# Pooled attention and a gated feed-forward in one program: sums of keys and values as one VectorE reduction, the last operands split on VectorE alone, tile 0's output by column halves, and an order that knows the shared SBUF port

## The chip, the cores and the metric

The kernel runs on one core of one Trainium2 chip. A core has TensorE (PE, matrix products into PSUM), VectorE (DVE), ScalarE (ACT), GpSimd (POOL, which has no access to PSUM here) and SyncE (SP, which issues the transfers). The metric is the device time of one execution in microseconds; smaller is better.

## The reference

```python
q, k, v: (8, 8, 576, 64) float32            # batch, heads, sequence, head dimension
k_p = k.reshape(B, H, 72, 8, D).mean(axis=3)  # keys and values pooled by 8
v_p = v.reshape(B, H, 72, 8, D).mean(axis=3)
scores = scale * q @ k_p.transpose(0, 1, 3, 2)
attn = softmax(scores)
x = (attn @ v_p) -> (4608, 512)              # tokens, heads x head dimension
g = x @ w_gate; val = x @ w_val              # (512, 1536) each
out = (g * sigmoid(g) * val) @ w_out         # (1536, 512)
```

All inputs and the output are float32. The weights come in as 64-bit floats and are turned into 32-bit ones on the chip. Products in 16-bit types run on a high part and a low part of each operand (three products for one).

## The kernel before

**Tiles and pieces.** The 4608 tokens form nine tiles of 512. The attention works on 40 pieces of at most 128 tokens of one batch. Tile 0 has pieces 0 to 3 and tile 1 pieces 4 to 8; batch 0 gives pieces 0 to 4.

**Keys and values.** Batch 0 is pooled on its own (keys by a reduction on VectorE, L405, values by products with a unit matrix, L510). For the batches 1 to 7, six parts each are loaded (`kv_part`, 576 KB, L1161), and GpSimd adds the eight addends of each result in three halving additions (L1169 to L1171). `prep` then scales and splits the values.

**A piece** (`answer`): scores on TensorE (L587), row maxima on VectorE (L594) and their scaled negative (`biases`, L598), eight exponentials on ScalarE with a running sum each (L606), the reciprocal (L613 to L616), a high part on ScalarE and a low part on GpSimd (`soft_low` L639 or `blocks_low` L649), a DMA transpose, the product with the values (L658 to L661 or L668 to L674), division (L678), again a high part on ScalarE and a low part on GpSimd (L1336), and a DMA transpose into the tile's x.

**Weights.** Each of twelve chunks of gate and value weights is decoded (`chunk`): a shift (L340), the sign (`w_sign`, on VectorE L352, GpSimd L347 or ScalarE L354), magnitude (L359), joining (L363), sums (L374), and a high and a low part (L389, L394).

**Steps.** A tile takes twelve steps, one per chunk. A plain step (`plain_step`, L771 to L773) multiplies 512 columns by both weights. A fast step (`fast_step`, L875) uses seven products of quarter blocks instead of eight, with 256 columns; it needs sums of weight blocks (`fast_weights`, L796 to L815) and of x (`fast_x`, L836 to L844). Tiles 0 and 1 are plain; from tile 2 on a chunk goes fast once its sums are made. The gate's tanh (L718) and two VectorE products (L721, L726) end a step, and the result goes to memory (L899).

**The output product** comes after the last tile. The intermediate comes back in blocks (L1469) and the product with `w_out` runs for pairs of tiles with seven products, called 1 to 7 (`last_products`), each of 2 x 18 matmuls of 512 columns: 6 with float32 operands rounded for the array (L1589) and 12 in bfloat16 with the low parts (L1603, L1604). Their left operands come from `operands`: block sums on VectorE (`less`, L1500, four sums of three parts each), and a cut of each operand into a rounded copy on ScalarE (L1486) and a low part (L1490), of which two parts of three are made on GpSimd and one on VectorE. Tile 0, the odd one, comes first (`single_operands`, `single_products`): four plain products of 2 x 18 matmuls.

**The order.** The order on every queue (TensorE, VectorE, ScalarE, GpSimd, SP) is written by a planner (`Order`) while the program is built. Every line of work is a generator that yields operations with an engine and a cost in ns, transfers with due times, buffers it takes (`get`) and puts back (`put`), and flags. The planner takes, of the operations that can start first, the one of the highest rank. Ranks come from a kind and a number; `CHUNK_RANK`, `KV_RANK`, `PIECE_RANK` and `VALUES` are such numbers for the beginning. The chip runs each queue in that order and waits where an operand is not ready.

Of the kernel before, what the change touches and what calls it, by code (L numbers as in the profile page):

```python
# [8 lines left out]
F16 = mybir.dt.float16  # L9
# [8 lines left out]
P = 128  # L18
# [5 lines left out]
LAG = 4  # L24
# [12 lines left out]
SIGN_AS_INT = (2, 4, 8, 9)  # L37
SIGN_ON_POOL = (5, 11)
# [28 lines left out]
class Order:  # L67
# [26 lines left out]
    def ready(self, e):  # L94
        return max(e["need"][4], self.pipe - self.HOLD if len(e["need"]) > 6 else 0)
# [50 lines left out]
    def run(self):  # L146
        while self.lines:
# [3 lines left out]
            for engine, free in self.free.items():  # L151
                ops = [e for e in self.lines if e["need"][0] == "op" and e["need"][1] == engine]
# [13 lines left out]
            _, engine, ns, f, _, *times = e["need"][:6]  # L166
            self.now = max(self.now, at)
# [27 lines left out]
def attention_then_swiglu(  # L195
# [71 lines left out]
    nc.gpsimd.memset(shares[:, 1:2], 1.0 / POOLW)  # L267
    least = const.tile([P, 4], F32, name="least")
# [73 lines left out]
    def w_sign(c):  # L342


        ws, high = chunks[c]["ws"], chunks[c]["high"]
        if c in SIGN_ON_POOL:
            nc.gpsimd.tensor_single_scalar(  # L347
                ws.bitcast(F16)[:, :, 1], high.bitcast(F32), 2.0**-60, ALU.mult
            )
        elif c in SIGN_AS_INT:  # L350
# [259 lines left out]

    def one_over(b, n, sm):
# [141 lines left out]
    def f_room(name):  # L753
# [7 lines left out]
            "hf": ["hf0", "hf1", "hh0", "hh1"], "rs": [0, 1], "f": [f_own], "xc": [(early, "early")],  # L761
# [23 lines left out]
    def fast_weights(c):  # L785

        if True:
            t = yield flag(("used", 1, c))
# [7 lines left out]
            t = yield op("DVE", 1280, lambda: nc.vector.tensor_add(f, g_h, g_l), t, t0)  # L796
# [23 lines left out]
    def fast_x(i):  # L820
# [9 lines left out]
        if i in SUMS_ON_POOL:  # L830
            on, eng, cost = nc.gpsimd, "POOL", (765, 1196)
# [972 lines left out]
```

## Time and profile before

| | us |
|---|---|
| median of 3 runs (lowest, highest) | 954.63 (953.04, 957.86) |
| the profiled execution | 950.87 |
| its span, first to last instruction | 948.8 |
| mean granted TensorE clock | 0.978 |
| first half step of tile 0 | 48.4 |
| first step of tile 1 | 143.6 |
| output product, from | 677 |

The span is the time from the first to the last instruction on the core. The share of busy time on the page is a mean over stages that differ much; the clock is what TensorE was granted, 1 being full. In a view by stretches, each row has the stretch, its length, the busy time and count for TensorE, its weight loads, VectorE, ScalarE and GpSimd, then the granted clock, the transfer engines' busy share and GB/s.

### The profile page before, as it was taken

What the parts mean: (1) busy time and instruction counts of PE and PEld (TensorE: products, weight loads), DVE (VectorE), ACT (ScalarE), POOL (GpSimd) and SP (SyncE); (2) the same over time, 40 slices, a digit from 0 to 9 for tenths busy, and PEclk for the clock granted to TensorE, in tenths of its full rate; (3) what the DMA queues carried; (4) which work ended last, traced back from release to release, by engine and by line L of the source; (5) the groups of instructions that cost most, each with busy time, mean ns of one, the idle gap of its engine ahead of it and who ended that gap; (6) DMA issues with size and microseconds to landing.
All of it is one profiled execution on the core that took longest, in us unless ns stands there. A gap on an engine that the chain in (4) does not pass through costs nothing. (4 is left out here: it accounts for less than half of the span.)

```text
span 948.8 us, 17997 instructions
## 1 busy us (share of the span) xinstructions
PE 887.7 (94%) x6687; PEld 628.9 (66%) x6687; DVE 666.6 (70%) x1016; ACT 539.4 (57%) x1408; POOL 584.0 (62%) x516
## 2 busy tenths in 40 slices
PE   4599889998999999998999999999899899999998
PEld 4486444445767887787888888888655455555554
DVE  5998966785885676865766655567737669496781
ACT  5899755553755664776676754455435345444442
POOL 3874997958829768648624513033547568677682
PEclk9699899999999999999999999999999899999999
DMA  9949974548359359469485543146450631706201
GB/s 328 329 144 277 249 168 102 127 132 194 83 163 184 104 137 261 119 164 252 103 170 142 127 123 112 67 145 234 178 176 3 224 131 54 289 12 251 104 23 67
DMA packets 138759, 148.38 MB, mean 156 GB/s; under 512 B 85808, under 2 KB 106288, under 8 KB 136368
## 3 DMA queue, kind: packets, MB, share of 16 engines
q1 hardware_dynamic: 138672, 147.24, 53.6%
q8 instruction: 52, 0.85, 0.4%
q14 instruction: 35, 0.29, 0.1%
HBM read 87.29 MB, written 40.89 MB: 135 GB/s over the span
## 5 line engine op out<-in xcount | busy, mean ns | idle before, releaser
L875 PEld LDWEIGHTS <-mixed 128*128 128x128 f16 x1404 | 136.4, 98 | 24.9 <-issue 5.5
L1603 PE MATMUL ps<-low,wsh 128*128 128x512 bf16 x384 | 146.7, 382 | 4.0 <-DVE low L1490 4.0
L875 PEld LDWEIGHTS <-wgv_h 128*128 128x128 f16 x1248 | 121.0, 98 | 32.5 <-issue 14.3
L875 PE MATMUL ps<-xc,mixed 128*128 128x256 f16 x936 | 123.2, 274 | 1.0 <-ACT ps L935 0.9
L875 PE MATMUL ps<-xc,wgv_h 128*128 128x256 f16 x624 | 109.6, 272 | 11.4 <-DVE ps L943 7.3
L721 DVE SCALAR_TENSOR_TENSOR hf<-hf,ps 128x512 f32<-128x512 f32 (+1 forms) x112 | 74.3, 664 | 63.0 <-ACT hf L718 62.6
L718 ACT ACTIVATE hf<-ps,un 128x512 f32<-128x512 f32 (+1 forms) x112 | 75.3, 672 | 72.3 <-PE ps L875 55.8
L606 ACT ACTIVATE sc<-ps,mx 128x72 f32<-128x72 f32 (+1 forms) x320 | 97.8, 330 | 22.2 <-DVE mx L598 19.4
L875 PE MATMUL ps<-x,wgv_h 128*128 128x256 f16 x624 | 109.2, 273 | 0.0
L726 DVE SCALAR_TENSOR_TENSOR hf<-ps,un,hf 128x512 f32<-128x512 f32 (+1 forms) x112 | 81.6, 729 | 37.8 <-PE ps L875 26.8
L771 PE MATMUL ps<-x,wgv_h 128*128 128x512 f16 (+1 forms) x272 | 98.3, 361 | 1.4 <-DMA x<-spare 1.4
L772 PE MATMUL ps<-x,wgv_h 128*128 128x512 f16 (+1 forms) x272 | 98.0, 360 | 0.5 <-DVE x L688 0.4
L773 PE MATMUL ps<-x,wgv_l 128*128 128x512 f16 (+1 forms) x272 | 97.8, 360 | 0.4 <-DVE wgv_l L394 0.3
L875 PE MATMUL ps<-x,wgv_l 128*128 128x256 f16 x312 | 85.1, 273 | 0.0
L875 PE MATMUL ps<-xc,wgv_l 128*128 128x256 f16 x312 | 85.0, 272 | 0.0
L649 POOL TENSOR_TENSOR half<-sc,half 128x448 f16<-128x448 f32 (+1 forms) x35 | 39.6, 1130 | 57.2 <-ACT half L644 51.2
L1490 POOL TENSOR_TENSOR low<-wgv_h,hs 128x1024 bf16<-128x1024 f32 x18 | 51.2, 2866 | 34.3 <-ACT hs L1486 34.3
L1603 PEld LDWEIGHTS <-wsh 128*128 128x128 bf16 x384 | 37.6, 98 | 51.5 <-issue 10.2
L1169 POOL TENSOR_TENSOR in<-in 128x576 f32<-128x576 f32 x42 | 62.3, 1483 | 13.8 <-DMA in<-kv_parts 13.8
L606 ACT ACTIVATION_READ_ACCUMULATOR sc<-ps,mx 128x1 f32 (+1 forms) x320 | 69.4, 217 | 0.0
L875 PE MATMUL ps<-x,mixed 128*128 128x256 f16 x468 | 64.1, 273 | 3.3 <-DVE ps L938 3.3
L875 PEld LDWEIGHTS <-wgv_l 128*128 128x128 f16 x624 | 61.0, 98 | 7.2
(189 smaller groups left out, 2095.3 us busy)
## 6 DMA issues: line engine op xcount, KB each, us to landing
hd<-hf SPq DMA_DIRECT2D x104, 256.0 KB, 2.3
in<-kv_parts SPq DMA_DIRECT2D x42, 576.0 KB, 5.4
ws<-w_all SPq DMA_DIRECT2D x36, 512.0 KB, 5.2
wgv_h<-hd SPq DMA_DIRECT2D x9, 1536.0 KB, 6.8
wgv_l<-hd SPq DMA_DIRECT2D x9, 1536.0 KB, 9.3
out_t<-ob SPq DMA_DIRECT2D x36, 256.0 KB, 3.8
qt<-q_rows SPq DMA_DIRECT2D x32, 256.0 KB, 3.5
wd<-wf SPq DMA_DIRECT2D x12, 256.0 KB, 2.4
```

The source lines that it names most:

```text
L606: nc.scalar.activation(sc[:n, h], pss[g][:n, j * SP : (j + 1) * SP], AF.Exp, bias=mx[:n, g, j : j + 1], scale=EXPSCALE, accum_out=sm[:n, h ...
L649: nc.gpsimd.tensor_sub(a[:, :, SP:], sc[:n, :, : P - SP], a[:, :, : P - SP])
L718: nc.scalar.activation(hf, gate, AF.Tanh, scale=un[:, c, 0:1])
L721: nc.vector.scalar_tensor_tensor(out=hf, in0=hf, scalar=1.0, in1=gate, op0=ALU.add, op1=ALU.mult)
L726: nc.vector.scalar_tensor_tensor(out=out, in0=val, scalar=un[:, c, 2:3], in1=hf, op0=ALU.mult, op1=ALU.mult)
L771: nc.tensor.matmul(o, wh, x["h"][:, j, a:e], start=(j == 0), stop=False)
L772: nc.tensor.matmul(o, wh, x["l"][:, j, a:e], start=False, stop=False)
L773: nc.tensor.matmul(o, wl, x["h"][:, j, a:e], start=False, stop=(j == NJ - 1))
L875: nc.tensor.matmul(o, a, b, start=begin and j + n == 0, stop=j == HJ - 1 and n == 2, skip_group_check=True,)
L1169: nc.gpsimd.tensor_add(a[:, :4], a[:, :4], a[:, 4:])
L1490: lambda: on.tensor_sub(low[:, 2 * n : 2 * n + 2], src[:, 2 * n : 2 * n + 2], rows[n].bitcast(F32)),
L1603: nc.tensor.matmul(o, top, where[1][:, c], start=False, stop=False, skip_group_check=True)
```

## The change

- **Sums of keys and values:** the three GpSimd additions of each of the 42 parts become one `tensor_reduce` on VectorE, and the host lays the eight addends next to each other.
- **Output operands:** all three low parts of every cut are made on VectorE.
- **Tile 0's output** goes through the same seven products as a pair, with its two column halves of 256 in place of the two tiles: 7 x 2 x 18 matmuls of 256 columns. Its operands share the two buffer sets by halves (`SLOT`). The first pair starts with product 3, which then has a bank of its own (`joined`).
- **The planner** treats VectorE operations marked `DVE+` and all GpSimd operations as exclusive of one another, and many costs are changed.
- **Attention:** 12 of the 40 pieces (`WHOLE`) subtract the row maximum and sum the rows on VectorE and take all exponentials in one ScalarE instruction. 19 low parts of the weights of attention and 13 low parts of x move from GpSimd to VectorE; the normalisation of all pieces of batch 0 is on GpSimd.
- **Beginning:** the values' loads have a rank of their own ahead of the chunks; new ranks for chunks, pieces and batch 1; five chunks instead of four in half steps for tile 0; the sign of six chunks on VectorE (before four), four on ScalarE (before six), two on GpSimd by `tensor_mul`; products of zeros on TensorE until the first step.
- Three chunks' low parts of weight sums move to VectorE, and the `w_out` cuts on VectorE are 4, 6 and 7 instead of 1, 7 and 3. The bank of the value sums goes to the attention and comes back at piece 8, and one more bank is lent at the end.

```diff
-LAG = 4
+LAG = 5
-SIGN_AS_INT = (2, 4, 8, 9)
-SIGN_ON_POOL = (5, 11)
+SIGN = dict(enumerate("DAAADAPPDDDD"))
-CHUNK_RANK = 0.9, 0.3
+CHUNKS = (1.08, 1.4, 1.95, 2.49, 2.66, 3.05, 3.37, 3.55, 3.86, 3.92, 4.12, 5.22)
-SECOND = 2
-BANKS = "val"
-VALUES = 0.9
+SECOND = 1
+BANKS = "att"
+VALUES = 0.47
+V_LOAD = 0.54
+WV = 9
+WHOLE = (0, 1, 3, 20, 21, 24, 25, 26, 28, 31, 34, 35)
-KV_RANK = 1.4
-PIECE_RANK = 0, 0.5, 1.2, 1.3, 2.2, 2.8, 3.4, 4, 4.6
-ON_POOL = (3, 4, 5, 6, 7, 8, 9)
+KV_RANK = 2.57
+CUT_ON_DVE = 0, 1, 2
+WAYS = {-1: (1, 5, 6, 2, 7, 3, 4), 0: (3, 1, 5, 2, 6, 7, 4)}
+SLOT = (0, 0), (0, 1), (1, 0), (1, 1), (0, 0), (1, 0), (1, 1)
+PIECE_RANK = (-0.26, 0.03, 1.27, 0.72, 1.85, 3.34, 3.35, 3.98, 3.19)
+ON_POOL = (0, 1, 2, 3, 4, 5, 6, 7, 8, 9)
+LOW_ON_DVE = (0, 4, 7, 12, 14, 15, 16, 19, 21, 23, 24, 26, 27, 28, 29, 32, 35, 37, 38)
+XT_ON_DVE = (0, 2, 3, 6, 7, 10, 13, 21, 24, 27, 30, 33, 38)
+WEIGHTS_ON_DVE = (1, 2, 8)
+CUT_W_ON_DVE = (4, 6, 7)
-SLACK = {"PE": 50, "DVE": 100, "ACT": 100, "POOL": 200, "SP": 100}
+SLACK = {'PE': 50, 'DVE': 100, 'ACT': 450, 'POOL': 50, 'SP': 100}
...
     def ready(self, e):
-        return max(e["need"][4], self.pipe - self.HOLD if len(e["need"]) > 6 else 0)
+        at = e["need"][4]
+        if e["need"][1] in ("DVE+", "POOL"):
+            return max(at, self.port - 200)
+        return max(at, self.pipe - self.HOLD if len(e["need"]) > 6 else 0)
...
+            if engine in ("DVE+", "POOL"):
+                self.port = at + ns - 160
...
+    def less_max(n, pss, sc, g):
+        mx = small.tile([P, GH], F32, name="mx1")
+        pv = pss[g][:n, : GH * SP].rearrange("p (h s) -> p h s", h=GH)
+        nc.vector.tensor_reduce(out=mx[:n], in_=pv, axis=AX.X, op=ALU.max)
+        nc.vector.tensor_tensor(
+            out=sc[:n].rearrange("p (j g) s -> p g j s", g=2)[:, g], in0=pv,
+            in1=mx[:n].unsqueeze(2).broadcast_to([n, GH, SP]), op=ALU.subtract,
+        )
+    def all_exponentials(n, sc):
+        nc.scalar.activation(sc[:n], sc[:n], AF.Exp, scale=EXPSCALE)
+    def row_sums(n, sc, sm):
+        nc.vector.tensor_reduce(out=sm[:n], in_=sc[:n], axis=AX.X, op=ALU.add)
...
     def fast_weights(c):
-            t = yield flag(("used", 1, c))
+            t = yield flag(("used", FAST_FROM - 1, c))
+            t = max(t, (yield flag(("decoded", 9 + c // 3 if c < 9 else c, 1))))
...
+    def warm():
+        where, t = yield get("val")
+        zeros = const.tile([P, TILE], F16, name="zeros")
+        t = yield op("POOL", 300, lambda: nc.gpsimd.memset(zeros, 0.0), 0)
+        def products():
+            ps = bank(where)
+            for _ in range(2):
+                nc.tensor.matmul(ps, zeros[:, :P], zeros, start=True, stop=True)
+        while ("taken", 0, 0) not in order.flags:
+            t = yield op("PE", 430, products, t)
+        put("val", where, t)
...
-            part["in"] = buffer(mid, [P, POOLW, KV // 6], F32, "in", "mid", at=n)
+            part["in"] = buffer(mid, [P, KV // 6, POOLW], F32, "in", "mid", at=n)
...
         def add():
-            a = part["in"]
-            nc.gpsimd.tensor_add(a[:, :4], a[:, :4], a[:, 4:])
-            nc.gpsimd.tensor_add(a[:, :2], a[:, :2], a[:, 2:4])
-            nc.gpsimd.tensor_add(dst, a[:, 0], a[:, 1])
-        t = yield op("POOL", 2800, add, t, ready)
+            nc.vector.tensor_reduce(out=dst, in_=part["in"], axis=AX.X, op=ALU.add)
+        t = yield op("DVE", 1400, add, t, ready)
...
     def cut_operand(p, k, src, t):
-            th = yield op("ACT", 1043, lambda: nc.scalar.copy(rows[n], src[:, 2 * n : 2 * n + 2]), t, t0)
-            eng, ns, on = (("POOL", 3000, nc.gpsimd), ("DVE", 2000, nc.vector))[n == 2]
+            na, nd, ng = (1043, 1210, 2390) if p >= 0 else (620, 680, 1270)
+            th = yield op("ACT", na, lambda: nc.scalar.copy(rows[n], src[:, 2 * n : 2 * n + 2]), t, t0)
+            eng, ns, on = (("POOL", ng, nc.gpsimd), ("DVE+", nd, nc.vector))[n in CUT_ON_DVE]
...
     def operands(p):
-        b11, b12, b21, b22 = (block[h, n] for h in range(2) for n in range(2))
+        if p < 0:
+            b11, b12, b21, b22 = (block[0, h][:, :, n * HT : (n + 1) * HT] for h in range(2) for n in range(2))
+        else:
+            b11, b12, b21, b22 = (block[h, n] for h in range(2) for n in range(2))
...
     def last_products(p):
-        for k in (1, 5, 2, 6, 3, 7, 4):
+        js = range(2) if p >= 0 else range(1)
+        def sides(j, o):
+            return [(j, o)] if p >= 0 else [(i, o[:, i * HT : (i + 1) * HT]) for i in range(2)]
+        turns = WAYS.get(p, WAY)
+        alone = turns.index(3) < turns.index(6)
+        for k in turns:
...
                 elif k in (6, 7):
                     o[j] = s[j]
+                    if k == 7:
+                        t0 = yield flag(("begun", p, 3, j))
...
-    kv = kv.reshape(B - SPLIT, POOLW, P, 6, -1).transpose(0, 3, 2, 1, 4)
+    kv = kv.reshape(B - SPLIT, POOLW, P, 6, -1).transpose(0, 3, 2, 4, 1)
```

More of the change, by code (lines that the diff above doesn't have):

```diff
@@ L151, in run @@
             for engine, free in self.free.items():
-                ops = [e for e in self.lines if e["need"][0] == "op" and e["need"][1] == engine]
+                ops = [e for e in self.lines if e["need"][0] == "op" and e["need"][1].rstrip("+") == engine]
                 if not ops:
@@ L1449, in operand_room @@
         low = const.tile([P, HC, TILE], BF16, name="low", tag="wo2", bufs=1)
-        put("set", (rows, low), t)
+        sets.append((rows, low))
+        order.done(("set", 0), t)
         t = yield flag(("tile", len(tiles) - 1))
@@ L1454, in operand_room @@
         low = const.tile([P, HC, TILE], BF16, name="low", tag="mixed2", bufs=1)
-        put("set", (rows, low), t)
+        sets.append((rows, low))
+        order.done(("set", 1), t)
+        if MORE:
+            where, t0 = yield get("val")
+            put("gate", where, t0)
     def load_block(p, h, n):
@@ L1479, in load_single, with room_for @@
         order.done(("block", -1, 0, n), t)
+    def room_for(p, k):
+        if p >= 0:
+            where, t = yield get("set")
+            return where, t
+        at = WAYS[p].index(k)
+        i, side = SLOT[at]
+        t = yield flag(("set", i))
+        if at > SLOT.index((i, side)):
+            t = yield flag(("made", p, WAYS[p][SLOT.index((i, side))]))
+        cs = slice(side * HT, (side + 1) * HT)
+        rows, low = sets[i]
+        return ([a[:, :, cs] for a in rows], low[:, :, cs]), t
     def cut_operand(p, k, src, t):
-        where, t0 = yield get("set")
+        where, t0 = yield from room_for(p, k)
         rows, low = where
@@ L1542, in operands @@
+        for k in WAYS.get(p, WAY):
+            src, when, free = of[k]
+            t = yield from cut_operand(p, k, src, (yield when))
             order.done(("cut", p, k), t)
-            if free:
+            if k == 3 and p >= 0:
+                order.start(("cut", p), freed(p, t))
+            elif free and p >= 0:
                 order.done(("free", p, *free), t)
+        if p < 0:
+            order.done(("free", p, 0, 1), max(t, (yield flag(("cut", p, 3)))))
     def seeded(p, k, j, o, src, t, t0):
@@ L1654, in last_products @@
             o = {}
-            for j in range(2):
+            for j in js:
                 t0 = 0
@@ L1735, in all_lines @@
             order.start(("load", -1), load_single(n))
-        order.start(("cut", -1), single_operands())
-        order.start(("out", -1), single_products())
+        order.start(("cut", -1), operands(-1))
+        order.start(("out", -1), last_products(-1))
         for p in range((len(tiles) - 1) // 2):
```

301 lines of the change are left out of this document (170 added, 131 removed).

## The prediction

> **What bounds the kernel now.** I read the page first, then the engines' busy time by stage, the waits of TensorE, and single lines for prices.
>
> ```profile
> span 948.8 us, 17997 instructions
> ...
> PE 887.7 (94%) x6687; PEld 628.9 (66%) x6687; DVE 666.6 (70%) x1016; ACT 539.4 (57%) x1408; POOL 584.0 (62%) x516
> ```
>
> The profiled execution took 950.87 us, 2.1 around its span; the median of the three runs is 954.63. I add my sum to the median. TensorE (PE) is busy 94% of the span, but that mean hides four stages. The next view gives busy time by stretch, then granted clock, DMA share and GB/s.
>
> ```profile
> 0.00:20.00 20.00, 8.44 (x50) 7.94 (x51) 10.44 (x29) 9.57 (x38) 6.89 (x26) 1.00 0.94 337
> 0.00:143.50 143.50, 109.59 (x816) 77.32 (x816) 119.78 (x228) 107.99 (x311) 102.66 (x125) 0.90 0.85 248
> 143.50:285.00 141.50, 134.80 (x1024) 81.30 (x1025) 105.13 (x178) 77.71 (x267) 97.77 (x116) 0.99 0.52 134
> 285.00:677.00 392.00, 380.73 (x3697) 326.43 (x3696) 258.69 (x500) 244.80 (x705) 204.85 (x217) 1.00 0.56 150
> 677.00:737.00 60.00, 60.00 (x270) 33.93 (x268) 37.51 (x22) 23.98 (x28) 37.95 (x14) 1.00 0.36 127
> 737.00:749.00 12.00, 8.00 (x27) 3.24 (x25) 9.30 (x8) 2.40 (x3) 4.95 (x2) 0.72 0.38 113
> 749.00:806.00 57.00, 56.72 (x253) 31.25 (x252) 44.60 (x27) 25.82 (x31) 41.04 (x15) 1.00 0.39 144
> ```
>
> The head (to 143.5, where tile 1 starts) leaves TensorE 33.9 us idle at a clock of 0.90, while VectorE (DVE) is busy 119.8, ScalarE 108.0, GpSimd (POOL) 102.7. To 285 TensorE idles another 6.7; from there to 677 it idles 11.3 of 392. From 677 the output product runs; it is TensorE's apart from one hole at 737 to 749.
>
> ```profile
> PE ps L875 <- DVE ps L943: 7.3, 10, 1.4
> ...
> PE ps L1603 <- DVE low L1490: 4.0, 1, 4.0
> PE ps L510 <- DMA vr<-v_left: 3.6, 1, 3.6
> PE ps L875 <- DVE ps L938: 3.3, 3, 2.6
> PE ps L875 <- DVE hf L726: 3.1, 3, 2.3
> ```
>
> The hole is one wait of 4.0 for a low part, and after it half clock (0.72 over 12 us, 3.4 us of clock). In the middle stage TensorE waits for VectorE (7.3 + 3.3 + 3.1).
>
> **Why VectorE and GpSimd are slow: the shared port.** These rows give shortest, median and longest instruction of a line.
>
> ```profile
> L1500 DVE TENSOR_TENSOR wgv_h<-wgv_h,wgv_l x12: 1211/3400/3421, 734.5 to 908.9; 128x1024 f32<-128x1024 f32 x12
> ```
> ```profile
> L1490 POOL TENSOR_TENSOR low<-wgv_h,hs x18: 2352/2832/3388, 672.3 to 929.8; 128x1024 bf16<-128x1024 f32 x18
> ```
> ```profile
> L726 DVE SCALAR_TENSOR_TENSOR hf<-ps,un,hf x112: 473/751/753, 54.7 to 677.9; 128x512 f32<-128x512 f32 x104, 128x256 f32<-128x256 f32 x8
> ```
>
> A VectorE subtraction with both inputs in SBUF takes 1.21 us or 3.4; a GpSimd one 2.35 or 3.4: one waits for the other's whole instruction. L726, with one input in PSUM, never goes over 0.753.
>
> **The change, part by part.**
>
> *Output product.* Per pair of tiles, seven operands are cut in three parts; before, GpSimd made two low parts (2.35) and VectorE one (1.21), and twelve sums run on VectorE: 7 x (2 x 2.35 + 1.21) + 12 x 1.21 = 55.9 us that cannot overlap, in a pair of 57.0. After: 33 x 1.21 = 39.9 on VectorE, GpSimd idle. So the hole goes: -4.0 - 3.4 = -7.4. What is late next is TensorE itself: the later pairs have 56.7 busy of 57.0. Both ends: 0 if another wait takes the place, -7.4.
>
> *Tile 0 by columns.* Before, 4 products x 36 matmuls of 512 columns; a pair has 252 of them in 57.0, 0.226 each, so 32.6 us. After, 7 x 36 = 252 of 256 columns: at half price 28.5, -4.1. The other end is the weight load of the 84 float32 matmuls:
>
> ```profile
> L1589 PEld LDWEIGHTS ps<-hs,wsh x204: 186/188/192, 677.0 to 938.6; 128*128 128x128 f32 x102
> ```
> ```profile
> 86.35 0.28 PE L308 MATMUL ps<-least,ones 128*128 128x2 f32 x2
> 86.49 0.36 PE L309 MATMUL ps<-wm,ones 128*128 128x2 f32 x2
> 86.71 0.38 PE L771 MATMUL ps<-x,wgv_h 128*128 128x512 f16 x1
> ```
>
> If each takes the recorded 0.188, tile 0 costs 84 x 0.188 + 168 x 0.113 = 34.8, +2.2. But four tiny float32 matmuls with their loads pass in 0.36 (86.35 to 86.71), 0.09 each, so loads are pipelined: I take -3.5. A rule speaks against it: the Trainium skill, TensorE: Matmul & The Clock Gate, Weight-path perf modes, gives float32 weights no fast load, and its LDWEIGHTS section gives columns / 1.2 GHz, an estimate of 107 ns for 128. By that rule the load just fits beneath a 256-column matmul and the gain stays; by the 188 row it is lost.
>
> Tile 0's 21 cuts and 12 sums at half size need 33 x about 0.68 = 22.4 us of VectorE inside 28.5 of TensorE, with the drains and pair 0's first operand: nearly full, and behind a late cut stand the sums of the next operand. I allow +2 (0 to +8). Product 7 now waits for 3's seed (a VectorE sum, like L726 at most 0.75), with the rest of TensorE's queue behind it; that is in the 2. Stores stay four, and the PSUM banks handed over earlier cost nothing. End stage: -7.4 - 3.5 + 2 = -9, ends -11.5 and +2.8.
>
> *Key and value sums.* Seven batches x six parts leave GpSimd for one VectorE reduction of 1152 elements to 144.
>
> ```profile
> L1169 POOL TENSOR_TENSOR in<-in x42: 1392/1403/2390, 18.5 to 460.2; 128x576 f32<-128x576 f32 x42
> L1170 POOL TENSOR_TENSOR in<-in x42: 789/794/1665, 20.0 to 461.7; 128x288 f32<-128x288 f32 x42
> L1171 POOL TENSOR_TENSOR box<-in x36: 485/488/1350, 89.4 to 462.5; 128x144 f32<-128x144 f32 x36
> ```
> ```profile
> L405 DVE TENSOR_REDUCE spare<-k 128x144 f32<-128x1152 f32 x1 | 2.2, 2227 | 0.9 <-DMA k<-k_rows 0.9
> ```
> ```profile
> L468 DVE TENSOR_REDUCE mx<-box x6: 701/742/743, 118.4 to 462.8; 128x1 f32<-128x576 f32 x6
> ```
> ```profile
> L594 DVE TENSOR_REDUCE mx<-ps x80: 397/448/458, 9.2 to 535.0; 128x4 f32<-128x288 f32 x64, 64x4 f32<-64x288 f32 x16
> ```
>
> GpSimd loses 2.69 a part. VectorE's price lies between L405, the same sizes read with a stride, 2.23, and the line through L594 and L468 (288 elements 0.448, 576 0.742, so about 1.33 at 1152). The new layout puts the eight in a row, as L468 reads: I take 1.35. The rule of the Trainium skill, VectorE: DVE Perf Modes, the TRN2 errata section, (58 + elements) / 0.96 GHz, would make it 1.26 as an estimate. The reductions (0.701 to 0.743, 0.397 to 0.458) show no trace of the port.
>
> *The rest of the attention and weight work, to 285 us.* Four batches (24 parts) were needed by then.
>
> ```profile
> L394 DVE SCALAR_TENSOR_TENSOR wgv_l<-mixed,sw,wgv_h 128x512 f16<-128x512 f32 x24 | 24.1, 1024 | 0.3 <-ACT wgv_h L389 0.2
> L363 DVE SCALAR_TENSOR_TENSOR mixed<-mixed,ws 128x1024 uint32<-128x1024 uint32 x12 | 18.3, 1527 | 2.0 <-POOL ws L347 1.8 <-ACT mixed L359 0.2
> ```
> ```profile
> L394 DVE SCALAR_TENSOR_TENSOR wgv_l<-mixed,sw,wgv_h x24: 731/827/1933, 34.3 to 128.1; 128x512 f16<-128x512 f32 x24
> ```
> ```profile
> L363 DVE SCALAR_TENSOR_TENSOR mixed<-mixed,ws x12: 1184/1252/2409, 21.9 to 120.9; 128x1024 uint32<-128x1024 uint32 x12
> ```
> ```profile
> L352 DVE TENSOR_SCALAR ws<-ws x4: 1317/1332/1884, 25.6 to 82.5; 128x1024 uint16<-128x1024 uint16 x4
> ```
> ```profile
> L844 DVE TENSOR_TENSOR xc<-fx,xc x8: 677/686/1000, 189.3 to 279.2; 128x512 f16<-128x512 f32 x8
> ```
>
> VectorE was busy 119.8 + 105.1 = 224.9 there. Added: 24 x 1.35 = 32.4; two more sign passes (six chunks for four) 2.7; four pieces whose softmax subtracts and sums on VectorE (two passes like L594 and one like L468, less one small bias) 4 x 1.45 = 5.8; five low halves 5 x 0.85, four x halves 4 x 0.69 and three weight chunks 3 x 1.5 (prices by L844) 11.5. The normalisations of pieces 0 to 2 go to GpSimd and the low halves of 0, 4 and 7 come from it: about equal, nil. Together 277.3.
>
> Taken off: waiting for the port. L394 and L363 lose 24 x 0.293 + 12 x 0.343 = 11.1 of their 42.4 us against their shortest. Some 40 steps (0.75 + 0.69 from PSUM) and the reductions of 20 pieces make about 78 us that do not wait; a quarter of the other 105 is 27; 38 in all, an estimate. GpSimd falls from 200.4 to some 108 (24 x 2.69, the halves, the signs), so half of it goes, -19. VectorE: 258 of 285.
>
> So this stage gets no lighter on VectorE; what gains is the order and GpSimd, which did 17 parts in the head (17 x 2.69 = 46 of its 102.7) ahead of the pieces that tile 1 waits for.
>
> ```profile
> 48.35 0.40 PE L771 MATMUL ps<-x,wgv_h 128*128 128x256 f16 x1
> ```
> ```profile
> 21.37 0.34 SPq L501 DMA_DIRECT2D vr<-v_left  x1
> ```
> ```profile
> 60.00:80.00 20.00, 19.67 (x200) 16.54 (x201) 19.34 (x44) 19.39 (x49) 7.46 (x12) 1.00 0.62 168
> ```
> ```profile
> 100.00:143.50 43.50, 34.36 (x223) 18.02 (x221) 35.00 (x62) 25.29 (x85) 41.69 (x42) 0.92 0.79 205
> ```
>
> The third value load, issued at 21.37, moves ahead of the chunks on SP's queue (keys, first queries and values are 3.2 MB, 9.5 us at 337 GB/s), so values can be pooled some 10 us sooner and the first step can come before 48.35. Chunk 0 waits behind 1.5 MB more, 4.5 us; who waits for it is VectorE, 10.44 of 20 busy there. Warming products of zeros go into TensorE's queue until the first step, two of 512 columns at a time: at most 2 x 0.226 in front of a real one. The head's lost clock (0.90, 14 us) I count at nothing: VectorE, not TensorE, covers it; if TensorE became the bound, it would be a gain. A fifth chunk in halves gives TensorE 24 matmuls (2.7 us) more before the second half of tile 0. The conversions' new wait for decoded chunks is nil: decoding ends at 128 (L394), before tile 1.
>
> With VectorE from 4.5 us on at share u, the 258 us end at 4.5 + 258/u: u = 0.92 gives 285 (no gain), 0.95 gives 276 (-9), 0.98 gives 268 (-17). It ran at 0.885 from 20 to 143.5 ((119.78 - 10.44) / 123.5) and 0.97 from 60 to 80. With GpSimd half empty I take 0.95: -9.
>
> *285 to 677.* VectorE gets 18 reductions (24), nine such softmaxes (13), low and x halves (some 20): 258.7 to about 305 of 392 after less waiting; TensorE stays the bound. Of its 11.3 idle I take half, -6 (0 to -9): GpSimd's share falls, so VectorE's drains come sooner.
>
> Sum: -9 - 6 - 9 = -24; 954.6 - 24 = 931.
>
> **The rivals.**
> 1. *The head does not move.* VectorE stays at 0.92: 0 - 6 - 9 = -15, 940. For it: VectorE carries as much as before. Against: GpSimd, full from 100 to 143.5 (41.69 of 43.5), is relieved.
> 2. *The order fits better.* 0.98 in the head (-17), -8, and an end stage at its bound of -11.5: -36, 918. For it: the 9.6 us of VectorE idle in the first 20, and 33.9 idle on TensorE.
> 3. *Slower: the reduction costs what L405 shows.* 24 x 0.88 = 21 more, 279; at 0.92 the stage ends at 308, +23, less 15: +8, 963. It decides from 271.9/0.92 = 295.5 + 4.5 = 300, where 258 + 24 x 0.57 is reached: 1.92 us a reduction. For it: same count of outputs; against: stride and L468.
> 4. *Tile 0 by columns loses* (0.188 loads): inside the forecast's end stage, +6.
>
> The Trainium skill, SBUF — State Buffer, Who interferes with whom, says that of VectorE and GpSimd the one that issues second is blocked until the first ends, and that a reduction never contends on trn2. The rows above agree (3.4 against 1.21; 0.743 at most).
>
> **How the numbers follow.** Forecast 0.50, rival 1 0.19, rival 2 0.22, rival 3 0.09. Half a per cent (950 to 959) is what a measurement tells from no change. Faster: 0.50 + 0.22 + most of rival 1 = 0.87; same 0.05; slower 0.08. The range leaves out rival 3 and the lower part of rival 2: 911 to 952.
>
> **What would show it.** Right: no instruction of L1490's successor on GpSimd, VectorE's operand sums all near 1.21, no wait of TensorE over 1 us in the output stage and full clock there; tile 0's output in 28 to 31 us; reductions near 1.35; first step before 40, tile 1 before 137. Wrong: reductions over 1.9; VectorE over 95% busy to 285 with TensorE waiting for it; float32 matmuls of 256 columns at 0.188; cuts late in tile 0's output.

## The result and the profile after

The changed kernel takes 923.3 us (920.04 to 925.87), the kernel before beside it 955.5 (953.04 to 957.86): a ratio of 0.966 with a 95% interval of 0.962 to 0.970. The forecast was 931 with a range of 911 to 952. Measured once more (last experiment) it took 925.1, a ratio of 0.971 (0.968 to 0.974); so two measurements of one kernel lie half a per cent apart, and less than that is not read as a difference below. The profiled execution took 924.83. One execution among all those below, of e9, took 1017 us at a lower clock and is left out.

The first lines of the page, then the busy time by stretch: stretch, length, busy time and count of TensorE (PE), its weight loads, VectorE, ScalarE and GpSimd, granted clock, DMA share, GB/s.

```profile
span 923.0 us, 18199 instructions
...
PE 888.3 (96%) x6895; PEld 638.7 (69%) x6895; DVE 733.3 (79%) x1203; ACT 519.7 (56%) x1244; POOL 254.3 (28%) x300
```
```profile
0.00:138.40 138.40, 119.32 (x879) 76.88 (x880) 115.93 (x238) 96.96 (x259) 43.58 (x72) 0.91 0.75 225
138.40:285.00 146.60, 141.98 (x1095) 87.35 (x1094) 129.95 (x214) 80.69 (x263) 101.35 (x113) 1.00 0.60 162
100.00:138.30 38.30, 37.92 (x259) 20.00 (x258) 34.34 (x63) 26.59 (x83) 7.84 (x14) 1.00 0.61 158
215.80:662.70 446.90, 437.80 (x4264) 372.12 (x4262) 357.15 (x665) 269.91 (x708) 160.63 (x176) 1.00 0.57 157
662.70:691.50 28.80, 28.80 (x254) 26.11 (x253) 23.69 (x37) 15.41 (x26) 0.00 (x0) 1.00 0.65 240
691.50:748.30 56.80, 56.80 (x256) 31.32 (x253) 46.18 (x43) 26.23 (x32) 0.00 (x0) 1.00 0.45 157
```

The span is 25.7 us shorter. TensorE's busy time hardly changed (887.7 before), but some 20 us of it are now products of zeros. So its own work takes less busy time than before: tile 0's output is shorter, and the mean granted clock rose from 0.978 to 0.987. The places, from the starts of TensorE's products in the two traces:

| | before | after | earlier or shorter by |
|---|---|---|---|
| first half step of tile 0 | 48.35 | 41.46 | |
| last product of tile 0 | 137.68 | 138.17 | |
| first of tile 1 | 143.58 | 138.39 | 5.2 |
| last of tile 1 | 221.09 | 215.67 | 5.4 |
| first of the output product | 677.02 | 662.75 | 14.3 |
| length of the output product, to its last matmul | 267.1 | 255.8 | 11.3 |
| of that, tile 0 | 32.2 | 28.8 | 3.4 |
| of that, the first pair | 63.2 | 56.8 | 6.4 |

**The head.** Tile 0 starts 7 us earlier and ends no earlier. What is gained is the gap behind it. TensorE's timeline and two stretches of the kernel before:

```profile
137.68 0.38 PE L773 MATMUL ps<-x,wgv_l 128*128 128x512 f16 x1
139.84 0.44 PE L587 MATMUL ps<-box,qt 64*128 64x72 f32 x2 [1.78 <-ACT sc L606]
141.03 1.11 PE L587 MATMUL ps<-box,qt 64*128 64x72 f32 x14 [0.76 <-ACT sc L606]
143.58 0.61 PE L771 MATMUL ps<-x,wgv_h 128*128 128x512 f16 x1 [1.44 <-DMA x<-spare]
```
```profile
100.00:137.70 37.70, 32.45 (x207) 16.76 (x205) 32.30 (x54) 21.27 (x64) 36.20 (x36) 0.91 0.80 202
137.70:143.60 5.90, 1.92 (x19) 1.28 (x18) 2.80 (x9) 4.12 (x21) 5.59 (x8) 0.97 0.76 220
221.20:677.00 455.80, 439.64 (x4214) 369.53 (x4212) 308.13 (x589) 280.91 (x821) 246.65 (x266) 1.00 0.56 149
```

Before, TensorE ran out of work at 137.7 and waited for tile 1's pieces; GpSimd was full (36.20 of 37.70, then 5.59 of 5.90). What the last piece of tile 1 waited for stands in the timeline of the kernel before:

```profile
137.96 0.62 ACT L1335 CAST spare<-sc 64x512 f16<-64x512 f32 x1 [4.40 <-DMA x<-spare]
138.33 0.79 POOL L1170 TENSOR_TENSOR in<-in 128x288 f32<-128x288 f32 x1
139.20 0.49 POOL L1171 TENSOR_TENSOR box<-in 128x144 f32<-128x144 f32 x1
139.65 1.15 POOL L1336 TENSOR_TENSOR spare<-sc,spare 64x512 f16<-64x512 f32 x1
140.82 1.23 SPq L1340 DMA_TRANSPOSE x<-spare  x1
```

The piece's high part (L1335) is done at 138.58, its low part (L1336) starts at 139.65, behind the rest of a sum of keys and values; its transpose lands at 143.53, and tile 1 starts at 143.58. The high part itself had waited for the buffer of the piece before, whose low part had started 2.2 us late behind another such sum (130.72 to 132.95). So 3.3 of the 5.9 us are low parts that stood behind sums on GpSimd. After, GpSimd has 7.84 of 38.30, the last transpose of tile 1 is issued at 132.17, 6.2 us ahead of its start, and from 100 us on TensorE itself is full (37.92 of 38.30).

**The middle** (tiles 2 to 8): TensorE's idle time falls from 455.8 - 439.6 = 16.2 to 446.9 - 437.8 = 9.1 us. **The output product** has no wait over 1.0 us and no half clock left.

TensorE's waits after (total, times, longest), and durations of single lines (shortest, median, longest):

```profile
PE ps L330 <- ACT wgv_h L394: 7.7, 2, 6.0
PE ps L911 <- DVE ps L980: 4.3, 7, 1.0
...
PE ps L911 <- DVE ps L975: 1.9, 2, 1.6
PE ps L911 <- DVE hf L761: 1.6, 4, 1.0
```
```profile
L1228 DVE TENSOR_REDUCE box<-in x36: 1304/1344/1355, 98.8 to 441.2; 128x144 f32<-128x1152 f32 x36
```
```profile
L1587 DVE TENSOR_TENSOR low<-wgv_h,more x33: 681/1219/1226, 668.7 to 905.4; 128x1024 bf16<-128x1024 f32 x30, 128x512 bf16<-128x512 f32 x3
```
```profile
L1597 DVE TENSOR_TENSOR wgv_h<-wgv_h,wgv_l x12: 1215/1218/1221, 721.0 to 883.2; 128x1024 f32<-128x1024 f32 x12
```

L1597 is the line whose median was 3400 ns before. The waits of the fast steps for VectorE went from 7.3 + 3.3 + 3.1 to 4.3 + 1.9 + 1.6.

### The profile page after: what moved, and what is told of

It reads as the page before. It is cut to its first block, busy times and chain, and to the rows that moved or that the text cites. A ratio compares the mean times of both kernels' runs of the same rounds, so it can differ in the third digit from the quotient of the medians.

```text
span 923.0 us, 18199 instructions
## 1 busy us (share of the span) xinstructions
PE 888.3 (96%) x6895; PEld 638.7 (69%) x6895; DVE 733.3 (79%) x1203; ACT 519.7 (56%) x1244; POOL 254.3 (28%) x300
## 4 chain that ended last, share of the span: by engine, by line
PE 73%; DVE 8%; DMA 3%; POOL 2%; issue 2%; ACT 2%; SPq 0%; DVEq 0%; ACTq 0%; POOLq 0%
PE ps L911 34%; PE ps L1707 10%; PE ps L1722 9%; PE ps L1721 9%; PE ps L607 3%; PE ps L806 2%; PE ps L808 2%; PE ps L807 2%; DMA in<-kv_parts 1%; DVE hf L761 1%; DVE hf L756 1%; DMA hd<-hf 1%; DMA pt<-half 1%; PE ps L709 1%; PE ps L708 1%
## 5 line engine op out<-in xcount | busy, mean ns | idle before, releaser
L1721 PE MATMUL ps<-low,wsh 128*128 128x512 bf16 (+1 forms) x420 | 146.2, 357 | 0.0
L753 ACT ACTIVATE hf<-ps,un 128x512 f32<-128x512 f32 (+1 forms) x113 | 75.5, 669 | 80.2 <-PE ps L911 59.4
L761 DVE SCALAR_TENSOR_TENSOR hf<-ps,un,hf 128x512 f32<-128x512 f32 (+1 forms) x113 | 81.6, 723 | 32.2 <-PE ps L911 24.9
L807 PE MATMUL ps<-x,wgv_h 128*128 128x512 f16 (+1 forms) x272 | 96.3, 354 | 0.4 <-DVE x L723 0.4
L806 PE MATMUL ps<-x,wgv_h 128*128 128x512 f16 (+1 forms) x272 | 96.4, 355 | 0.0
L626 ACT ACTIVATE sc<-ps,mx 128x72 f32<-128x72 f32 (+1 forms) x224 | 68.6, 331 | 17.8 <-DVE mx L618 17.8
L1721 PEld LDWEIGHTS <-wsh 128*128 128x128 bf16 x420 | 40.6, 97 | 45.5 <-issue 7.6
L876 POOL TENSOR_TENSOR fx<-fx 128x256 f32<-128x256 f32 x56 | 43.8, 783 | 61.2 <-DVE fx L872 56.2
L970 ACT COPY rs<-ps 128x256 f32<-128x256 f32 x79 | 29.5, 374 | 45.3 <-PE ps L911 31.7
L1722 PE MATMUL ps<-hs,wsl 128*128 128x512 bf16 (+1 forms) x156 | 54.6, 361 | 0.0
L1722 PE MATMUL ps<-more,wsl 128*128 128x512 bf16 (+1 forms) x144 | 51.8, 368 | 0.0
```

Source lines behind the costliest of these rows:

```text
L626: nc.scalar.activation(sc[:n, h], pss[g][:n, j * SP : (j + 1) * SP], AF.Exp, bias=mx[:n, g, j : j + 1], scale=EXPSCALE, accum_out=sm[:n, h ...
L753: nc.scalar.activation(hf, gate, AF.Tanh, scale=un[:, c, 0:1])
L761: nc.vector.scalar_tensor_tensor(out=out, in0=val, scalar=un[:, c, 2:3], in1=hf, op0=ALU.mult, op1=ALU.mult)
L806: nc.tensor.matmul(o, wh, x["h"][:, j, a:e], start=(j == 0), stop=False)
L807: nc.tensor.matmul(o, wh, x["l"][:, j, a:e], start=False, stop=False)
L876: t1 = yield op(eng, cost[0], lambda: on.tensor_sub(o, a, b), t1)
```

## The experiments

The theory after the result: the output stage gained by its cut (all low parts on VectorE); the head and the middle gained because GpSimd was relieved of the sums, so that VectorE no longer waits for the port. The rival for head and middle: the order (ranks, and the planner's knowledge of the port) did it, and the moved work by itself does little.

Each run's median and ratio to the kernel before (953.3 to 953.8 us in these comparisons, 955.5 in the first row's), and from its trace, in us:

| | median | ratio, 95% interval | tile 1 from | output from | its length |
|---|---|---|---|---|---|
| changed kernel | 923.3 | 0.966 (0.962 to 0.970) | 138.4 | 662.8 | 255.8 |
| e1, no zeros | 925.7 | 0.970 (0.968 to 0.972) | 138.7 | 664.5 | 255.7 |
| e2, fewer zeros | 921.9 | 0.967 (0.965 to 0.968) | 136.0 | 658.9 | 255.8 |
| e3, sums on GpSimd | 943.9 | 0.990 (0.987 to 0.993) | 159.2 | 681.1 | 255.8 |
| e4, two cuts of three on GpSimd | 941.0 | 0.988 (0.984 to 0.991) | 136.9 | 661.9 | 271.7 |
| e5, before with all cuts on VectorE | 944.9 | 0.991 (0.988 to 0.994) | 147.5 | 679.5 | 260.5 |
| e6, before with sums on VectorE | 950.0 | 0.997 (0.995 to 0.998) | 147.0 | 677.3 | 267.4 |
| e7, planner without the port | 939.1 | 0.985 (0.981 to 0.989) | 144.0 | 678.5 | 256.2 |
| e8, pieces as before | 919.6 | 0.965 (0.961 to 0.968) | 140.8 | 657.9 | 255.6 |
| e9, strided reduction | 941.1 | 0.988 (0.985 to 0.991) | 141.3 | 675.0 | 255.8 |
| e10, no joint exponentials | 926.5 | 0.972 (0.970 to 0.974) | 146.0 | 664.1 | 255.6 |
| e11, e8 with fewer zeros | 928.7 | 0.974 (0.972 to 0.977) | 145.1 | 668.4 | 255.6 |
| e12, changed kernel again | 925.1 | 0.971 (0.968 to 0.974) | 138.7 | 662.3 | 255.8 |

In e5 and e7 the first output products run ahead of the end of the last fast step, so "its length" holds some 0.7 us of that step. Tile 1's start comes from one profile each. In e5 every engine runs the same instructions in the same order as in the kernel before until the output stage, and yet its tile 1 starts at 147.5 instead of 143.6. So a difference of that size against the old order is not read below, and the 5.2 us by which tile 1 starts earlier are known no better. The changed kernel's order, which e4 and e12 have up to the output stage and e1 has but for the zeros, gave 136.9 to 138.7.

### The products of zeros: e1 and e2

The prediction allowed a zero product to stand "at most 2 x 0.226" in front of a real one. TensorE's timeline, the zeros' line, and VectorE's timeline of the changed kernel:

```profile
20.99 1.87 PE L607 MATMUL ps<-spare,qt 64*128 64x72 f32 x16 [2.36 <-DMA qt<-q_rows]
22.80 6.60 PE L1188 MATMUL ps<-zeros 128*128 128x512 f16 x14
29.23 0.28 PE L329 MATMUL ps<-least,ones 128*128 128x1 f32 x2
29.37 0.36 PE L330 MATMUL ps<-mx,ones 128*128 128x1 f32 x2
```
```profile
29.77 0.16 DVE L335 TENSOR_SCALAR p2s<-ps 128x1 uint32<-128x1 uint32 x1 [4.07 <-PE ps L330]
```
```profile
22.80:28.16 5.36, 5.08 (x12) 1.29 (x12) 2.87 (x6) 4.16 (x23) 2.16 (x2) 0.50 0.75 240
```

Fourteen zero products take 29.23 - 22.80 = 6.43 us: ten at half clock (0.50 in the stretch above, 0.54 us each), then four at full clock in the other 1.07 us, 0.27 each. The queue ran in the written order, so the values' scale came late, and VectorE waited 4.07 us for it.

e1 leaves the zeros out:

```diff
-        order.start(("early", 99), warm())
```

> The changed kernel without the products of zeros on TensorE before the first step; nothing else is altered, only the order is planned again. Theory (the zeros stand in front of the values' total, whose maximum was ready at 21.7 us while the total ran at 29.2, behind 14 products at half clock): total of the values at 22 to 24 us, first half step at 34 to 38 instead of 41.5, tile 1 from 132 to 136 instead of 138.4, time 917 to 921. Rival (the zeros keep the clock up, and decoding on ScalarE and VectorE sets the head): first step at 41 to 45, tile 1 at 138 to 142, time 923 to 928.

e2 lets the planner count a pair at 860 ns, so that it writes fewer (44 for 58):

```diff
-            t = yield op("PE", 430, products, t)
+            t = yield op("PE", 860, products, t)
```

> The changed kernel with the same products of zeros, but each pair of them planned at 860 ns, what a pair takes at half clock, instead of 430. Theory (the harm is that the queue was planned at full clock and ran at half): about half as many zeros, total of the values at 22 to 26 us, time 917 to 921, like the kernel without them or a little better since the clock stays up. Rival (decoding sets the head): tile 1 from 137 to 140, time 922 to 925.

The time up to the first step, in the changed kernel and in e1:

```profile
0.00:41.40 41.40, 34.99 (x226) 19.43 (x227) 29.42 (x73) 18.63 (x49) 14.87 (x34) 0.92 0.86 284
```
```profile
0.00:40.50 40.50, 23.23 (x168) 21.41 (x168) 29.55 (x73) 19.05 (x49) 15.31 (x34) 0.83 0.91 290
```

Without the zeros VectorE has the values' scale at 27.55 instead of 29.77, so they cost it 2.2 us. The first step comes at 40.5 instead of 41.5, far from the theory's 34 to 38, and tile 1 at the same 138.7; with fewer zeros, at 39.9 and 136.0. All three times lie within the half per cent. e1's time is in its rival's range, e2's in neither. The zeros do keep the clock up: it is half from 21.3 to 28.2 us with them and from 26.4 to 43.5 without, while every queue otherwise has the same instructions in the same order. But neither the 2.2 us nor the clock shows in the time.

### The sums of keys and values: e3 and e6

e3 puts them back on GpSimd (old layout, three additions) and keeps the rest:

```diff
-            nc.vector.tensor_reduce(out=dst, in_=part["in"], axis=AX.X, op=ALU.add)
+            a = part["in"]
+            nc.gpsimd.tensor_add(a[:, :4], a[:, :4], a[:, 4:])
+            nc.gpsimd.tensor_add(a[:, :2], a[:, :2], a[:, 2:4])
+            nc.gpsimd.tensor_add(dst, a[:, 0], a[:, 1])
-        t = yield op("DVE", 1400, add, t, ready)
+        t = yield op("POOL", 2690, add, t, ready)
```

> The changed kernel with the sums of the 42 parts of keys and values back on GpSimd as three additions, in the old layout. Theory (GpSimd and the port it shares held back the x of the tiles from tile 1 on): the 113 us of additions come back, VectorE's two-input operations wait again, and 8 to 16 us of the gain before the output product are lost, time 931 to 939. Rival (VectorE's added 56 us just replaced GpSimd's work): VectorE gets lighter as GpSimd gets heavier, time 921 to 926.

It loses some 20 us, more than expected, and all of it ahead of tile 1 (159.2 for 138.4), in tile 0's steps (38.9 to 159.0), where the theory had named the x of tile 1 and later. Two stretches of e3, the waits of ScalarE from 40 to 160, and a piece of GpSimd's timeline:

```profile
100.00:120.00 20.00, 15.31 (x80) 7.12 (x81) 15.74 (x20) 6.99 (x13) 19.22 (x19) 0.88 0.91 260
120.00:140.00 20.00, 14.63 (x82) 6.76 (x80) 14.92 (x22) 11.05 (x43) 19.21 (x20) 0.84 0.64 211
```
```profile
ACT hf L753 <- POOL un L1072: 7.9, 3, 5.3
...
ACT hf L753 <- POOL in L1230: 4.3, 1, 4.3
```
```profile
130.06 0.20 POOL L1067 TENSOR_TENSOR p2w<-p2w 128x1 f32<-128x1 f32 x1
130.21 1.41 POOL L1229 TENSOR_TENSOR in<-in 128x576 f32<-128x576 f32 x1
131.69 1.12 POOL L1230 TENSOR_TENSOR in<-in 128x288 f32<-128x288 f32 x1
132.89 0.75 POOL L1231 TENSOR_TENSOR box<-in 128x144 f32<-128x144 f32 x1
133.60 0.24 POOL L1072 TENSOR_TENSOR un<-p2w,mt 128x3 f32<-128x3 f32 x1
```

The step's tanh on ScalarE (L753) needs `un`, a 0.2 us product on GpSimd, and it stands behind a whole sum, 3.4 us here. Until the tanh is done the step's bank isn't free. So the price is not only the sums' own time: in the new order of ranks they stand in front of what a step waits for. The waits shown are 12 us; how much of the 20 they make, the runs don't tell. The kernel before has the same `un` on GpSimd (L1035) and no wait of ScalarE for it in its head; its ranks placed the sums otherwise, in front of the low parts shown above.

e6 is the other side: the kernel before, with the reductions (and their layout) alone.

```diff
-            a = part["in"]
-            nc.gpsimd.tensor_add(a[:, :4], a[:, :4], a[:, 4:])
-            nc.gpsimd.tensor_add(a[:, :2], a[:, :2], a[:, 2:4])
-            nc.gpsimd.tensor_add(dst, a[:, 0], a[:, 1])
+            nc.vector.tensor_reduce(out=dst, in_=part["in"], axis=AX.X, op=ALU.add)
-        t = yield op("POOL", 2800, add, t, ready)
+        t = yield op("DVE", 1400, add, t, ready)
```

> The kernel before, with one other part alone: the sums of keys and values as one VectorE reduction of eight neighbours, in the old order of ranks. Theory (the sums are most of what the head gained): GpSimd loses 46 us of the head's 102.7 and VectorE's waits for the port go (24 us in the head by a tally against the shortest of each kind), so tile 1 starts at 130 to 139 in place of 143.6, the rest stays, 940 to 949. Rival: the reductions by themselves only load VectorE (17 x 1.35 = 23 us in the head) and the gain needs the new ranks: tile 1 at 143 to 155, 953 to 966.

```profile
0.00:147.00 147.00, 112.86 (x800) 78.84 (x800) 123.19 (x237) 106.99 (x304) 45.52 (x74) 0.86 0.78 233
```

GpSimd falls from 102.7 to 45.5 us in the head, as meant, and the gap behind tile 0 shrinks from 5.9 to 2.3 us (144.7 to 147.0). But tile 0's steps, from 46.2 on, take 98.5 us instead of 89.3, and tile 1 starts no earlier. Neither range holds the time (950.0); tile 1's start is in the rival's. Relieving GpSimd alone gives 0.3% in all, while e3 loses 2% without it: the sums on VectorE gain only together with other parts of the change. e7 below takes out one of these parts; the new ranks were not tried by themselves.

### The output operands' cut: e4 and e5

e4 gives two of three low parts of each cut back to GpSimd:

```diff
-CUT_ON_DVE = 0, 1, 2
+CUT_ON_DVE = (2,)
```

> The changed kernel with two of three low parts of the output operands back on GpSimd, the third on VectorE; tile 0 still goes by columns and the planner still knows the port. Theory (55.9 us a pair that cannot overlap, against 56.7 of TensorE): a hole of some 4 us comes back in the output stage, with half clock behind it, and TensorE waits in tile 0's part too: output stage 263 to 270 us instead of 255.8 to the last matmul, time 930 to 938. Rival (a planner that knows the port works around it): output stage 256 to 259, time 923 to 926.

Two of its stretches (each a pair of tiles), a wait of TensorE, and the sums' line:

```profile
690.60:750.90 60.30, 58.21 (x256) 32.33 (x260) 43.23 (x28) 25.13 (x30) 41.15 (x14) 1.00 0.39 144
750.90:814.60 63.70, 58.63 (x254) 32.02 (x258) 46.74 (x29) 25.68 (x31) 40.61 (x14) 1.00 0.42 154
```
```profile
PE ps L1721 <- DVE low L1587: 4.9, 4, 2.1
PE ps L1707 <- DVE ps L1682: 4.8, 3, 1.6
```
```profile
L1597 DVE TENSOR_TENSOR wgv_l<-wgv_l x12: 1211/3397/3408, 707.5 to 891.5; 128x1024 f32<-128x1024 f32 x12
```

Up to the end of tile 0's output e4 runs as the changed kernel does (output from 661.9, tile 0's part 28.8). Then every pair loses, 16 us in all, more than expected (271.7 for 263 to 270): a VectorE sum again takes 3.4 us when it meets a GpSimd low part, and TensorE waits for a low part or for a sum of products (L1682) behind it.

e5 does the cut's part alone in the kernel before:

```diff
-            eng, ns, on = (("POOL", 3000, nc.gpsimd), ("DVE", 2000, nc.vector))[n == 2]
+            eng, ns, on = ("DVE", 1210, nc.vector)
```

> The kernel before, with one part of the change alone: all three low parts of each output operand's cut on VectorE (tile 0 stays in four plain products, keys and values stay on GpSimd). Theory: the 4.0 us wait, the half clock behind it and the port's waits belong to the low parts on GpSimd; the first pair falls from 63.2 to about 57, the head and the middle stay (tile 1 from 143.6, output from 677), tile 0's output stays at 32: 953.4 - 7 = 944 to 948. Rival: VectorE now carries 33 passes of 1.21 us and the drains in each pair and its order leaves a wait of its own: first pair 60 to 64, 950 to 956.

```profile
712.30:769.20 56.90, 56.86 (x254) 31.32 (x253) 40.98 (x39) 25.81 (x31) 0.00 (x0) 1.00 0.41 148
```

The first pair takes 56.9 instead of 63.2, and the time falls by 8.4 us. This part stands by itself, as forecast.

### What the planner knows: e7

The order is planned as if VectorE and GpSimd were independent; the work is the same.

```diff
-        if e["need"][1] in ("DVE+", "POOL"):
+        if False:
```

> The changed kernel, where the planner takes VectorE and GpSimd as independent, as it did before. The work is the same, only the order may differ. Theory: with GpSimd at 254 us of 923 the two seldom meet, the planner's knowledge is worth little: 922 to 928, tile 1 between 137 and 142, VectorE's waits for the port in the head still under 10 us. Rival: the order with the port is what makes the head short: tile 1 at 143 to 150, 929 to 937, with VectorE's two-input rows longer by 10 us and more in the head.

```profile
221.70:680.00 458.30, 443.77 (x4253) 372.69 (x4250) 362.54 (x662) 268.41 (x703) 162.01 (x174) 0.99 0.55 151
```

It loses 14 to 16 us (939.1 against 925.1 and 923.3), more than the rival had: 5.6 up to tile 1, the rest in tiles 2 to 8, where TensorE idles 458.3 - 443.8 = 14.5 us instead of 9.1 and is busy 6 us more, part of it at half clock (234.4 to 241.2). The theory falls: taken out of the changed kernel, this condition of the planner costs more than the output stage gained. It is not waiting for the port that grows most, as the rival had it: by a tally of every VectorE instruction over the shortest of the same line and shape, the excess in the first 145 us is 12.5 us against 7.9, and 26.2 in the kernel before. So the loss is rather what stands behind the late ones in the queues; which of them, the runs don't tell.

One rival is left: the ranks came with a planner that knew the port, and another order may lose just by not fitting them. The other runs that were planned anew (e2, e8, e10, e11) moved the time by 6 us at most, so chance alone is an unlikely reason for 14; what the condition gives in the kernel before was not tried.

### VectorE's load: e8, e10, e9

e8 takes the attention's changes out, e10 only the first of the three.

```diff
-WHOLE = (0, 1, 3, 20, 21, 24, 25, 26, 28, 31, 34, 35)
+WHOLE = ()
-LOW_ON_DVE = (0, 4, 7, 12, 14, 15, 16, 19, 21, 23, 24, 26, 27, 28, 29, 32, 35, 37, 38)
-XT_ON_DVE = (0, 2, 3, 6, 7, 10, 13, 21, 24, 27, 30, 33, 38)
+LOW_ON_DVE = ()
+XT_ON_DVE = ()
```

> The changed kernel with the attention's pieces as before: no piece takes all its exponentials at once, and no low part of a weight or of x is made on VectorE (all on GpSimd). VectorE loses some 42 us (12 x 1.45 + 19 x 0.85 + 13 x 0.69), about 12 of them in the head, GpSimd gains about 32 low parts. Theory: what bounds the head is VectorE with its waits for GpSimd; what it loses in work comes back as waits for the port: tile 1 at 138 to 145, 923 to 932. Rival: VectorE's own work is the bound: tile 1 at 130 to 136, 915 to 921.

> The changed kernel, where no piece takes all its exponentials in one ScalarE instruction (12 pieces go back to eight exponentials with a running sum each); the low parts on VectorE stay. Theory: the twelve softmaxes cost VectorE 12 x 1.45 = 17 us that nobody waits for and free ScalarE of work that is not the bound: same within error, 919 to 925. Rival: ScalarE's relief is what makes the head and TensorE's waits for the exponentials short: 926 to 932, with TensorE waiting for exponentials again (7 us and more in the kernel before).

```profile
PE 889.8 (97%) x6897; PEld 638.6 (70%) x6897; DVE 695.4 (76%) x1131; ACT 543.2 (59%) x1424; POOL 290.3 (32%) x348
```

The line is e8's page. VectorE does 38 us less than in the changed kernel (695.4 for 733.3), GpSimd 36.0 and ScalarE 23.5 more, and the time is 0.4 to 0.6% shorter than the changed kernel's two measurements, which is at the edge of what they can tell: 919.6 is in the rival's range, tile 1's start (140.8) in the theory's. For e10 the time (926.5, in the rival's range) is no different from the changed kernel's by their intervals, while its tile 1 starts at 146.0, and TensorE does not wait for the exponentials as the rival had it (1.7 us at most for a line of them). So no theory is settled here; what is shown is that 38 us of VectorE's work, moved to GpSimd and ScalarE, change the time by 6 us at most, and that this part of the change did not bring the gain.

e9 keeps the one reduction, with the old layout:

```diff
-            nc.vector.tensor_reduce(out=dst, in_=part["in"], axis=AX.X, op=ALU.add)
+            nc.vector.tensor_reduce(
+                out=dst, in_=part["in"].rearrange("p t n -> p n t"), axis=AX.X, op=ALU.add
+            )
```

> The changed kernel with the eight addends of a sum a stride of 144 elements apart, as the kernel before stored them, and read through that stride by the same one reduction; nothing else differs. Theory: L405's 2.23 us in the kernel before is the price of the stride, so 36 reductions cost 2.2 each in place of 1.34, 0.88 x 24 = 21 us more of VectorE by 285 us; VectorE has 39 us idle there, so the head and the stage to 285 lose part of it: 928 to 938. Rival: the number of results sets the price and L405's length is of another cause, reductions near 1.35, 921 to 926.

```profile
L1228 DVE TENSOR_REDUCE box<-in x36: 2060/2093/2139, 100.4 to 453.1; 128x144 f32<-128x1152 f32 x36
L1228 DVE TENSOR_REDUCE spare<-in x6: 2076/2119/2147, 38.7 to 64.7; 128x144 f32<-128x1152 f32 x6
```

The stride is the price: 2.09 us for 1.34, for the same sums. 42 x 0.75 = 31.5 us more on VectorE cost 16.0 us (941.1 against 925.1 beside it), more than expected, spread over head, tile 1 and tiles 2 to 8 (tile 1 +2.9, output +12.3 in the profiles). That 38 us less gave 6 at most and 31 us more cost 16 fits an order written for 1.4 us, which every queue of e9 keeps: work that the planner knows of is placed, work that runs over its planned time is waited for. That e9's loss would shrink with 2.1 in the plan was not tried.

### A version put together: e11, and e12

e11 joins the edits of e8 and e2, whose medians were the lowest (the three lists empty, a pair of zeros at 860).

> A version put together from two runs: pieces as in the kernel before (all low parts of weights and x on GpSimd, no joint exponentials) and half as many zero products (the planner counts 860 ns a pair in place of 430, about their length at half clock). Theory: both small gains add (-4 and -1 to -3 of the changed kernel's time): 914 to 919. Rival: each is within the spread of orders that the planner finds, not a gain of a mechanism: 918 to 925.

> The changed kernel once more, on the same chip as the version put together from two runs, so that the two can be compared. Both theories: 920 to 926.

At 928.7 against 925.1 beside it, with intervals that overlap, it is no better, and worse than both expectations (e12 is in its own); the small gains of e2 and e8 don't add up. They are of the size by which orders differ from each other (tile 1 starts at 145.1 here, at 136.0 and 140.8 in the two that it joins). No run beat the changed kernel by more than its measurement can tell.

## Why the prediction was right, step by step

The sum was -24 and the span became 25.7 shorter. That the total came so close is in part luck: the head gave less than forecast in these two profiles, by another way than its sum had it, and the middle and the output stage gave more.

| step | forecast | measured |
|---|---|---|
| head (put to 285 us; measured at tile 1's end) | -9 | -5.4 |
| from there to the output product | -6 | -8.9 |
| output stage | -9 | -11.3 |

- **The hole in the output stage**, -7.4: the first pair gave 6.4; e5 alone made the output product 6.6 shorter and gave 8.4 in time. Right, place and size; GpSimd stands at 0.00 there, L1597 at 1.22.
- **Tile 0 by columns**, 28.5 us: 28.8. The float32 row below has 12 loads in 1.49 us, 0.124 each and not 0.188, as the four tiny products had shown. By the Trainium skill (TensorE: Matmul & The Clock Gate, LDWEIGHTS section) a float32 load is an estimate of 107 ns; the loads fit nearly beneath the products, and the gain stayed, as that rule had it. The recorded 0.188 is how long one load takes, not how far apart they start.
- **The +2 for late cuts**: nothing of it came. 23.69 us of VectorE fit into 28.80 without a wait. The stage ended at the bound that the prediction had kept for rival 2.
- **The reduction**, 1.35: 1.344. Rival 3's price (2.23) is that of the stride, as argued; but its turning point was wrong: with 2.09 the kernel (e9) is still 1.2% faster than before, where the prediction had it turn slower from 1.92.
- **The head's model failed.** It let 258 us of VectorE work end at a share of 0.95. Up to 285 us VectorE did 115.93 + 129.95 = 245.9, a share of 245.9 / 280.5 = 0.88. At 0.88 its 258 us would have ended near 298, 13 us later than before, and yet tile 1 ended 5.4 us earlier: VectorE's total did not set the end. (In the kernel before, its share was 224.9 / 280.5 = 0.80.) What gained was the gap behind tile 0, where low parts stood behind sums on GpSimd. The prediction's words had that (sums "ahead of the pieces that tile 1 waits for"), its sum had not. "What gains is the order and GpSimd" was half right: GpSimd alone (e6) gives 0.3%, and the planner's knowledge of the port, taken out (e7), costs 14 to 16 us. The prediction listed that knowledge as part of the change and gave it no price of its own. A small slip beside it: 4 and 9 softmaxes were added where `WHOLE` lists 12 pieces, 1.45 us too much.
- **Waiting for the port**, -19 on VectorE to 285: by the tally above it fell from 49.9 to 32.0, so -18. Right in size, but not worth its length in time.
- **The middle**, half of 11.3: right in kind, larger in size: in tiles 2 to 8 idle time fell by 7.1 us and busy time by 1.8, about what 3.4 us at half clock had cost there (443.6 to 447.0, before).
- **Signs**: first step before 40: no, 41.46, and still 40.5 without the zeros (e1), so they are not the whole reason. The prediction had them at full clock and two at a time; fourteen stood in front of a real product, ten of them at half clock. Tile 1 before 137: no, 138.4. Tile 0's output in 28 to 31, no wait over 1 us there: yes.

```profile
670.97 1.67 PE L1707 MATMUL ps<-more,wsh 128*128 128x256 f32 x12
672.48 0.29 PE L1721 MATMUL ps<-low,wsh 128*128 128x256 bf16 x1
```
```profile
670.94 1.49 PEld L1707 LDWEIGHTS ps<-more,wsh 128*128 128x128 f32 x12
```

(TensorE's timeline and that of its weight loads, changed kernel.)

The median fell by 32 us where the span fell by 25.7, because the profiled execution of the kernel before (950.87) was one of its shorter ones; e5's profile, with the same order, is 3.9 us longer up to tile 1.

## What to carry to other kernels

Price a move off the shared port where it is a chain of its own, with one engine waiting for one operand: there the trace of before gives the answer (hole, full clock, drains). In a stage that a planner orders, busy shares don't give a price: look for the gap in the bounding engine and what stands in front of the instruction that ends it, and don't expect moved work to pay without an order that knows its true durations and the port. Test such a change from both sides, the part alone in the old kernel and undone in the new: here the two gave 0.3% and 2%.

## What the runs showed of the hardware

- A reduction of eight neighbours against one of eight elements 576 bytes apart: 1.34 against 2.09 us, with equal counts of inputs and results. The Trainium skill, VectorE: DVE Perf Modes, the TRN2 errata section, gives (58 + elements) / 0.96 GHz, an estimate of 1.26 for both, without a term for the stride; the same section says that this row comes out below measured durations, and 1.34 lies above it too. The Trainium skill, SBUF — State Buffer, section "Door 1: The DMA port swizzle", says that each access that crosses to a new 16-byte line pays a penalty; the measured difference agrees in sign.
- The reduction shows no trace of the port in the changed kernel (1304 to 1355 ns over 36), though 24 of all 42 ran beside a GpSimd instruction. A VectorE sum of the output stage, with two inputs in SBUF, took 1.22 us with GpSimd idle and 3.4 beside a GpSimd low part (e4).
- Products of zeros brought the granted clock back and held it: after 5.4 us of them it rose from half to full at 28.2 us and stayed up to 48.6. Without them (e1) it was half from 26.4 to 43.5. That gained nothing that the time shows.
